# Pacing of weight loads, filler products, narrowing order and MLP piece counts in a DeltaNet + SiLU MLP kernel

## The chip, the cores and the metric

The kernel runs on one core of a Trainium2 chip. Its time is the device time of one execution in microseconds (us); the number given for a kernel is the median of its runs. A core has five engines that work side by side, each through its own instructions in order: TensorE (PE, matrix products; the loads of the stationary operand are shown as PEld), VectorE (DVE), ScalarE (ACT), GpSimd (POOL) and SyncE (SP), which here only issues DMA transfers. The engines wait for each other through semaphores. PE, DVE and ACT meet in PSUM, eight banks that PE writes; everything else lies in SBUF.

## The reference

Two blocks follow each other. The first is a delta rule over 768 tokens, for 4 batches of 8 heads of dimension 48:

```python
k_n = k / (norm(k) + 1e-6)
for t in range(S):
    y[t]  = q[t] @ state
    v_old = state.T @ k_n[t]
    state = state + beta[t] * outer(k_n[t], v[t] - v_old)
```

Its output, as 3072 rows of 384, goes through an MLP: `h = x @ w_in` (384 to 2048), `g = h * sigmoid(h)`, `out = g @ w_out` (2048 to 384). The two weights arrive as 64-bit floats, 6.3 MB each.

## The kernel before, in words

**Chunks.** The 768 tokens are cut into six chunks of 128. In a chunk the recurrence becomes matrix algebra: keys and queries are transposed (`turn`, L412), their products are taken (`score`, L438), a triangular matrix per head is inverted, and then the chunk is solved in two halves (`solve`: `keys`, `inner`, `update`, `old`, `new`, lines L650 to L779). The inversion of chunk 0 (`invert_first`, L549 to L625) works on 16x16 corners on DVE (17 steps, two instructions each), transposes them with DVE and joins them by 32x32 products on PE (L583, L603, L618); that of the later chunks (`invert`, L513/L518) is 31 steps on DVE, after a way through DRAM (`block_out`, `block_in`) and with another one behind it (`low`, `up`, read back by L531 and L100).

**The MLP as filler.** The products of the MLP for chunk c are generators (`feed_forward`: `hidden` L847 and, for chunk 0, `project` L877, later `combine` L944). `run(n)` takes n pieces from them. The main loop calls `run` between the steps of the next chunk's preparation, inversion and solution, so that PE has work while other engines hold up the recurrence. How many pieces stand where is written out by hand.

**Narrowing.** Weights are fetched as pairs of 32-bit words, in 16 pieces of 128x768 doubles (`fetch_w_in` L243, `fetch_w_out` L255), into rooms that are used for something else before or after. `narrow` (L176 to L201) makes a piece into fp32: two ACT instructions (L182, L183), when the piece is begun; then three DVE steps, L187 (maximum), L190 (shift and mask) and L194 (sign), and behind the third one POOL addition (L198). `fill(n)` does the next n of these DVE steps, in the order of a queue of pieces; a piece's ACT instructions are issued by `begin`.

**Order.** Every instruction is pinned behind the one before it on its engine (`pin`), DMA issues on SP too (`in_line`): what a program line issues first runs first on its engine, and what waits holds up all that stands behind it. `behind(a, b, Sync)` makes a wait for b's completion.

**Fillers without a result.** `busy(n)` (L289) issues n products of 128x128 by 384 columns into a bank named `pw` that nobody reads; each shows as two matmul records. `read` (L754) is a copy of eight columns of an accumulating bank, which the next products into that bank wait for.

Of the kernel before, what the change touches and what calls it, by code (L numbers as in the profile page):

```python
# [21 lines left out]
def kernel(  # L22
# [19 lines left out]
    W = 64  # L42
# [26 lines left out]
    def behind(later, earlier, how=NoSync):  # L69

        tc.add_manual_dep(
            later.ins, earlier.ins.name,
            mybir.DependencyInfo(how, mybir.DependencyReason.DATA), reason="order",
        )
# [3 lines left out]
    def pin(op):  # L78

        engine = op.ins.engine  # L80
        if engine in pins:
            behind(op, pins[engine])
        pins[engine] = op
        return op

    line = []

    def in_line(dma):

        if line:  # L90
            behind(dma, line[-1])
        line.append(dma)
        return dma

# [7 lines left out]
    def go(steps, n=1):  # L102
        for _ in range(n):
            next(steps, None)
# [34 lines left out]
    def load_k(c, bs=ALL):  # L139
        if c < NCH:  # L140
            load_pair(kbufs[c % 2], k, c, bs)
# [13 lines left out]
                    ))  # L155

    seen = const.tile([P, 1], FP32, name="seen")
    pin(nc.vector.memset(seen[:], 0.0))
    for t in (kbufs[0], zbuf, kbufs[1]):
        for h in range(2):  # L160
            pin(nc.vector.memset(t[:, 2 * h : 2 * h + 2, :, :, D:W], 0.0))
# [15 lines left out]
    def narrow(to, raw):  # L177

        low, high = raw[..., 0], raw[..., 1]
        bits = to.bitcast(U32)  # L180
        across = "p a f -> p f a"
        pin(nc.scalar.activation(out=to, in_=high.bitcast(FP32), func=ACTF.Abs))  # L182
        pin(nc.scalar.activation(  # L183
            out=low.bitcast(I32), in_=low, func=ACTF.Identity, scale=2.0**-29, bias=plus23[:]
        ))
        yield
        yield pin(nc.vector.tensor_scalar(  # L187
            out=to.rearrange(across), in0=to.rearrange(across), scalar1=LOW_HIGH, scalar2=None, op0=ALU.max
        ))
        yield pin(nc.vector.tensor_scalar(  # L190
            out=bits.rearrange(across), in0=bits.rearrange(across), scalar1=3, scalar2=0x3FFFFFFF,
            op0=ALU.logical_shift_left, op1=ALU.bitwise_and,
        ))
        done = pin(nc.vector.scalar_tensor_tensor(  # L194
            out=bits, in0=high, scalar=0xC0000000, in1=bits,
            op0=ALU.bitwise_and, op1=ALU.bitwise_or,
        ))
        pin(nc.gpsimd.tensor_tensor(  # L198
            out=to.bitcast(I32), in0=to.bitcast(I32), in1=low.bitcast(I32), op=ALU.add
        ))  # L200
        yield done  # L201
# [88 lines left out]
    def busy(n=1, after=None, how=NoSync):  # L290

        for _ in range(n):
            pw = bank(CC, "pw")
            done = pin(nc.tensor.matmul(
                pw[:, 0:DM], lhsT=ident[:],
                rhs=states[0][:].rearrange("p u a w -> p (u a w)")[:, 0:DM], start=True, stop=True,
            ))
            if after is not None:
                behind(done, after, how)
                after = None  # L300
# [4 lines left out]
    def beta_of(c):  # L305
        pb = bank(A, "pb")
        pin(nc.tensor.transpose(
            pb[:, 0:BH], beta_fm[:, c].rearrange("n s t -> n (s t)"), ident[0:BH, 0:BH]
        ))
        pin(nc.scalar.activation(  # L310
            out=beta_tok[:, c, :].rearrange("p (n e) -> p e n", e=2),
            in_=pb[:, 0:BH].rearrange("p (e n) -> p e n", e=2), func=ACTF.Copy,
        ))
# [15 lines left out]
    def add_squares(c, b):  # L329

        pin(nc.vector.tensor_reduce(
            out=sums[c][:, b * H : (b + 1) * H], in_=squared[c, b // HB][:, b % HB], axis=AX.X, op=ALU.add
        ))
# [150 lines left out]
    def block_in(c):  # L484
        there, g, _ = blocks[c]
        in_line(nc.sync.dma_start(out=g, in_=there[:]))
# [257 lines left out]
    def old(c, g, hf):  # L744

        py = pys[g] = bank(A, "pyc")
        for u, p, e, _, of, to in of_heads():
            yield pin(nc.tensor.matmul(  # L748
                py[to, C * p + W * u : C * p + W * (u + 1)],
                lhsT=states[g][of, u, p, :], rhs=kqs[c, g * HB + u][of, p, 1, on(e, hf)],  # L750
                start=p == 0 and u == 0, stop=False, skip_group_check=True,
            ))
        if hf == 1:
            pin(nc.vector.tensor_copy(out=read[:], in_=py[:, 0 : 512 : W]))  # L754

    def new(c, g, hf):

# [247 lines left out]
    class Piece:  # L1005
# [3 lines left out]
        def begin(self):  # L1009
            if self.steps is None:  # L1010
                kind, i = self.name
                self.steps = (narrow_w_in if kind == "in" else narrow_w_out)(i)
                next(self.steps)
# [6 lines left out]
    def fill(n):  # L1020

        for _ in range(n):
            if not queue:
                return
            piece = queue[0]
            piece.begin()
            last = next(piece.steps)
            piece.done += 1
            if piece.done == 3:
                narrowed.append(piece.name)  # L1030
                queue.popleft()
                for i in freed:
                    fetch_w_out(i)
                freed[:] = {
                    ("in", 4): [2], ("in", 5): [3], ("in", 6): [4], ("in", 7): [6], ("out", 0): [7], ("out", 1): [5]
                }.get(piece.name, [])
                for next_up in list(queue)[:2]:
                    if next_up.name in raws:
                        next_up.begin()
        return last  # L1040

    def until(name):
# [31 lines left out]
    def first_queries(b):  # L1074

        def evacuate(j, e, to, of):
            by_act(to, of)

        turn(0, b, 1, M)
        score(0, b, (1,), (A, CC), evacuate)  # L1080

    block_in(0)
    for b in range(2):
        first_queries(b)
    for _ in norm_steps(0):
        pass
    for t in xis:
        pin(nc.gpsimd.memset(t[:], 0.0))
    step = block_steps(0)
    pin(nc.gpsimd.memset(spread[:], 0.0))  # L1090
    for i in range(3):
        fetch_w_in(i)
    for c in range(1, NCH):
        beta_of(c)
    for b in range(2, B):
        first_queries(b)
    for i in range(3):
        begin(("in", i))
    inv = invert_first(step)
    for n in range(1 + Q):  # L1100
        done = next(inv)
        if n in (4, 7, 10, 13):
            busy(1, done, Sync)
    go(inv)
    load_v(0)
    for g in range(2):
        size(0, g)
    for i in (3, 4):
        fetch_w_in(i)
    load_k(1)  # L1110
    for i in (5, 6):
        fetch_w_in(i)
    fill(4)
    go(inv)
    fill(3)
    go(inv)
    fill(1)
    go(inv)
    fetch_w_in(7)
    fill(1)  # L1120
    assert next(inv, 0) == 0

    def masks(g):
        for u in range(HB):
# [28 lines left out]

    def lengths(c):

        for b in range(B):
            square(c, b)
            if b % HB == 1:
                for x in (b - 1, b):
                    add_squares(c, x)  # L1160
                yield
        yield from norm_steps(c)

    def prepare(c):
# [31 lines left out]
    for n in range(5):  # L1196
        go(solving)
        if n in (1, 2):
            masks(n - 1)
        if n > 2:  # L1200
            for b in (0, 1):
                turn(1, 2 * (n - 3) + b, 0, M)
        fill((1, 1, 1, 1, 2)[n])
        busy(1)
    long = lengths(1)
    for n in range(5):
        go(solving)
        run(2)
        if n == 0:
            for i in (0, 1):  # L1210
                fetch_w_out(i)
        fill(2)
        go(long, 2 if n < 2 else 6)
    assert next(solving, 0) == 0
    go(long, 99)
    load_v(1)
# [20 lines left out]
    for c in range(1, NCH):  # L1237
        solving = solve(c)
        long = lengths(c + 1) if c + 1 < NCH else iter(())
        for n in range(6):  # L1240
            go(solving)
            run()
            if n >= 2:
                go(long, 4)
        run(999)
        pieces = chained(feed_forward(c, 0), feed_forward(c, 1))
        needed = iter(())
        go(long, 99)
        for n in range(3):
            go(solving)  # L1250
            run()
            if c == 1:
                go(sums_made)
        assert next(solving, 0) == 0
        if c + 1 < NCH:
            step = block_steps(c + 1)
            for n, _ in enumerate(prepare(c + 1)):
                run(2 if n == 0 else 3 if n == 1 else 1)
                if n == 2:
                    load_v(c + 1)  # L1260
            run(3)
            for n, _ in enumerate(invert(c + 1, step)):
                if n % 7 != 3:
                    run()
                if n == 3:
                    load_k(c + 2)
            run(9)
# [31 lines left out]
```

## Time and profile before

| | |
|---|---|
| runs of the kernel | 757.7, 758.02 and 759.09 us, median 758.02 |
| profiled execution | 760.12 us, of which the profile's span is 758.1 us |
| busy: PE, PEld | 709.8 us (94%), 617.4 us (81%) |
| busy: DVE, ACT, POOL | 414.0 us (55%), 203.8 us (27%), 88.2 us (12%) |
| chain that ended last | PE 70%, DVE 11%, DMA 4% |

Instructions that only issue a DMA, branch or count a semaphore are not in the busy times. A matmul of fp32 is shown as two records, each with a weight load. The granted clock is the share of the full TensorE clock that the core had. In lists of waits the columns are: who waited for whom, microseconds in total, how often, the longest. In timelines: start, duration, engine, line, operation, and in brackets the idle time of the engine just before it and what ended it. In tables by stretch: the stretch and its length, the busy time of PE, PEld, DVE, ACT and POOL with instruction counts, the granted clock, the DMA engines' share and GB/s.

### The profile page before, as it was taken

Reading aid. Unit: us, or ns where it says so; the run is one execution under the profiler, and the core shown is the slowest. Engines: PE = TensorE matmul, PEld = TensorE weight load, DVE = VectorE, ACT = ScalarE, POOL = GpSimd, SP = SyncE. Lnnn points to the kernel's source line nnn. Section 1 sums busy time; section 2 is a strip of 40 time slices with the busy share of each in tenths; the row PEclk is TensorE's granted clock in tenths of the full one; section 3 lists DMA queues with packets and bytes.
Section 4 is the critical chain, followed back from the end, with each engine's and each line's share of the span. In section 5 each row is a group of like instructions: output and inputs, shape, how many; then the busy total and the mean of one; then the engine's idle time right before and its main releaser. Section 6 shows DMA issues by size and latency. Waiting matters only on the chain.

```text
span 758.1 us, 21218 instructions
## 1 busy us (share of the span) xinstructions
PE 709.8 (94%) x9394; PEld 617.4 (81%) x9394; DVE 414.0 (55%) x942; ACT 203.8 (27%) x417; POOL 88.2 (12%) x86
## 2 busy tenths in 40 slices
PE   5779996799999999999999999999999999999996
PEld 4557784476787999897999897999897999989996
DVE  5856877997454493544593543593543593321212
ACT  3514444221233212223212233112233112231110
POOL 4231514600102000102000102000102000000000
PEclk9655999999999999999999999999999999999999
DMA  8951538502117504017504017504017104010000
GB/s 117 283 129 40 169 54 223 83 22 65 32 30 96 91 22 84 3 39 94 94 22 84 6 39 102 84 22 85 6 39 101 42 22 85 9 38 1 22 0 22
DMA packets 149131, 49.25 MB, mean 65 GB/s; under 512 B 134880, under 2 KB 142176, under 8 KB 149040
## 3 DMA queue, kind: packets, MB, share of 16 engines
q1 hardware_dynamic: 146928, 47.63, 31.7%
q8 instruction: 74, 1.21, 0.6%
q10 hardware_dynamic: 2112, 0.26, 0.3%
q14 instruction: 17, 0.14, 0.1%
HBM read 33.91 MB, written 11.80 MB: 60 GB/s over the span
## 4 chain that ended last, share of the span: by engine, by line
PE 70%; DVE 11%; DMA 4%; issue 1%; POOL 1%; ACT 1%; SPq 0%; DVEq 0%; ACTq 0%; POOLq 0%
PE phid L847 27%; PE px L944 14%; PE py L944 9%; PE pyc L761 3%; DMA z<-in_q_dram 3%; PE pa L438 3%; PE pu L707 2%; PE pyc L748 2%; PE ph L675 2%; PE pt L412 2%; PE po L877 2%; PE pz L687 2%; DVE w_out L190 2%; DVE rank L513 2%; DVE x L518 2%; PE px L650 1%
## 5 line engine op out<-in xcount | busy, mean ns | idle before, releaser
L847 PE MATMUL phid<-xT,w_in 128*128 128x256 f32 x1152 | 263.3, 384 | 0.0
L847 PEld LDWEIGHTS phid<-xT,w_in 128*128 128x128 f32 x1152 | 215.8, 191 | 32.3 <-issue 2.8
L857 ACT ACTIVATE gT<-phid 128x512 f32<-128x512 f32 x96 | 57.3, 597 | 193.0 <-PE phid L847 181.3
L513 DVE SCALAR_TENSOR_TENSOR rank<-g,step,x 128x31 f32<-128x31 f32 (+15 forms) x155 | 62.2, 401 | 28.5 <-DMA g<-blocks 24.0
L927 DVE TENSOR_TENSOR sums_of_g<-gT 128x384 f32<-128x384 f32 (+1 forms) x60 | 32.7, 567 | 58.0 <-ACT gT L857 47.3
L944 PE MATMUL px<-sums_of_w,sums_of_g 128*128 128x192 f32 x320 | 58.2, 331 | 0.0
L518 DVE TENSOR_TENSOR x<-x,rank 128x31 f32<-128x31 f32 (+15 forms) x155 | 54.7, 353 | 5.7
L944 PE MATMUL py<-w_out,sums_of_g 128*128 128x192 f32 x320 | 55.3, 326 | 0.0
L944 PEld LDWEIGHTS px<-sums_of_w,sums_of_g 128*128 128x128 f32 x320 | 51.9, 190 | 0.9
L944 PEld LDWEIGHTS py<-w_out,sums_of_g 128*128 128x128 f32 x320 | 52.5, 190 | 0.0
L877 PE MATMUL po<-w_out,gT 128*128 128x384 f32 x128 | 46.0, 505 | 5.5 <-POOL w_out L198 5.5
L327 POOL TENSOR_TENSOR sq<-kb 128x384 f32<-128x384 f32 x24 | 20.5, 876 | 246.8 <-PE px L650 229.4
L687 PEld LDWEIGHTS pz<-vf,xi 64*64 64x64 f32 x768 | 39.8, 141 | 9.3 <-issue 7.1
L687 PE MATMUL pz<-vf,xi 64*64 64x48 f32 x768 | 42.6, 224 | 4.5 <-DVE nt L354 3.8
L448 DVE TENSOR_TENSOR ap<-pa,above 128x256 f32<-128x256 f32 x40 | 15.1, 418 | 51.8 <-ACT ap L453 51.8
L456 DVE COPY xT<-pyc 32x128 f32<-32x128 f32 (+2 forms) x66 | 18.7, 284 | 44.4 <-ACT xT L453 44.4
L877 PEld LDWEIGHTS po<-w_out,gT 128*128 128x128 f32 x128 | 23.7, 194 | 22.5 <-POOL w_out L198 8.0
L438 PE MATMUL pa<-kq 48*64 48x128 f32 (+1 forms) x896 | 29.7, 278 | 7.6 <-ACT kq L422 7.3
L438 PEld LDWEIGHTS pa<-kq 48*64 48x64 f32 x896 | 23.7, 147 | 14.0 <-ACT kq L422 9.0
L748 PE MATMUL pyc<-kq,state 48*64 48x64 f32 x704 | 35.0, 223 | 0.0
L748 PEld LDWEIGHTS pyc<-kq,state 48*64 48x64 f32 x704 | 32.1, 134 | 3.4 <-issue 3.4
L675 PEld LDWEIGHTS ph<-state,kq 48*64 48x64 f32 x704 | 26.7, 134 | 5.0 <-issue 3.8
(159 smaller groups left out, 922.3 us busy)
## 6 DMA issues: line engine op xcount, KB each, us to landing
vf<-in_v_dram SPq DMA_DIRECT2D x24, 192.0 KB, 5.2
out_dram<-o SPq DMA_DIRECT2D x48, 96.0 KB, 2.2
sums_of_w<-in_moe_w_out_dram SPq DMA_DIRECT2D x5, 768.0 KB, 6.2
w_out<-in_moe_w_in_dram SPq DMA_DIRECT2D x4, 768.0 KB, 7.8
blocks<-ap SPq DMA_DIRECT2D x44, 64.0 KB, 1.9
g<-blocks SPq DMA_DIRECT2D x5, 512.0 KB, 3.7
up<-x SPq DMA_DIRECT2D x5, 512.0 KB, 4.0
xi<-up SPq DMA_DIRECT2D x40, 64.0 KB, 2.6
```

What stands on the lines that cost most here:

```text
L438: pin(nc.tensor.matmul(pa[e][half, p * n * W : (p + 1) * n * W], lhsT=kq[rows, p, 0, half], rhs=kq[rows, p, js[0] : js[-1] + 1, half], sta ...
L513: pin(nc.vector.scalar_tensor_tensor(out=tv, in0=g[:, 0:m, m : m + 1].to_broadcast([P, m, n]), scalar=step[:, m : m + 1], in1=x[:, m : m + ...
L518: yield pin(nc.vector.tensor_tensor(out=x[:, 0:m, m:T], in0=x[:, 0:m, m:T], in1=tv, op=ALU.add))
L675: yield pin(nc.tensor.matmul(ph[on(e, hf), n * D : (n + 1) * D], lhsT=kqs[c, g * HB + u][of, p, 0, on(e, hf)], rhs=states[g][of, u, p, 0:D ...
L687: yield pin(nc.tensor.matmul(pz[rows, n * D : (n + 1) * D], lhsT=xis[g][rows, u * H + 2 * p + e, :], rhs=vfs[c][rows, hf, g * HB + u, p, : ...
L748: yield pin(nc.tensor.matmul(py[to, C * p + W * u : C * p + W * (u + 1)], lhsT=states[g][of, u, p, :], rhs=kqs[c, g * HB + u][of, p, 1, on ...
L761: yield pin(nc.tensor.matmul(py[to, C * p + W * u : C * p + W * (u + 1)], lhsT=zbuf[rows, g * HB + u, hf, p, :], rhs=aps[c, g][rows, 1, u, ...
L847: pin(nc.tensor.matmul(ph[:, j * GT : (j + 1) * GT], lhsT=w_in[:, a, (2 * f + j) * P : (2 * f + j + 1) * P], rhs=xTs[c, hf][:, a, :], star ...
L857: pin(nc.scalar.activation(out=gTs[f // FG][:, f % FG, :], in_=ph[:], func=ACTF.Silu, scale=0.5))
L877: pin(nc.tensor.matmul(po[n][:, 0:DM], lhsT=gTs[f // 2 // FG][:, f // 2 % FG, at : at + C], rhs=w_outs[f // HFF][:, f % HFF, :], start=(f ...
L927: pin(nc.vector.tensor_tensor(out=sums_of_g[:, k, fs], in0=of[0], in1=of[1], op=op))
L944: pin(nc.tensor.matmul(to, lhsT=at, rhs=quarter(f, *b) if isinstance(b, tuple) else sums_of_w[b][:, f], start=start and f == 0, stop=f == ...
```

## The change

The lines of the kernel after are one or a few higher than those of before.

- Pacing: `in_line` can make a DMA wait for a DVE instruction (`pace`, filled by `paced`). The chunk-0 values `load_v(0)` go ahead of the weights; `w_in` pieces 2 and 3, the keys of chunk 1 and `w_in` pieces 4 to 7 each wait on SP for the DVE instruction that was last issued at that place. Before, three pieces, the values, two pieces, the keys and two more pieces stood one after another.
- Filler products: four after `block_in(0)`, one after each query block, one ahead of the third; six instead of four beside the chunk-0 inversion, each waiting for a DVE step.
- The scaling of the values (`size`, POOL L397) waits for the DVE instructions that follow the first join (L593).
- Narrowing: L187 and L190 go over the piece in memory order instead of across its rows; `in` 1 and 2 are begun after the inversion; a next piece is begun when the piece ahead has done its first DVE step, instead of two at once when one ends. Fills stand at other places beside the chunk-0 joins.
- `read` is copied by ACT instead of DVE. The squares of a chunk's keys (`lengths`) are taken in two groups, their sums one step later, and in chunk 0's solution the steps of `lengths(1)` come later.
- From chunk 1 on: `run` takes two pieces instead of one in two steps of the solution, three instead of two in the first step of the preparation, and 24 instead of 27 beside the inversion.

```diff
-    line = []
+    line, pace = [], []
     def in_line(dma):
         if line:
             behind(dma, line[-1])
+        if pace:
+            behind(dma, pace.pop(), Sync)
         line.append(dma)
         return dma
...
-    pin(nc.vector.memset(seen[:], 0.0))
+    seen_on = pin(nc.vector.memset(seen[:], 0.0)).ins.engine
...
-        across = "p a f -> p f a"
...
         yield pin(nc.vector.tensor_scalar(
-            out=to.rearrange(across), in0=to.rearrange(across), scalar1=LOW_HIGH, scalar2=None, op0=ALU.max
+            out=to, in0=to, scalar1=LOW_HIGH, scalar2=None, op0=ALU.max
         ))
         yield pin(nc.vector.tensor_scalar(
-            out=bits.rearrange(across), in0=bits.rearrange(across), scalar1=3, scalar2=0x3FFFFFFF,
+            out=bits, in0=bits, scalar1=3, scalar2=0x3FFFFFFF,
...
         if hf == 1:
-            pin(nc.vector.tensor_copy(out=read[:], in_=py[:, 0 : 512 : W]))
+            by_act(read[:], py[:, 0 : 512 : W])
...
-                for next_up in list(queue)[:2]:
-                    if next_up.name in raws:
-                        next_up.begin()
+                if queue and queue[0].name in raws:
+                    queue[0].begin()
+            elif piece.done == 1 and len(queue) > 1 and queue[1].name in raws:
+                queue[1].begin()
...
     block_in(0)
+    busy(4)
     for b in range(2):
         first_queries(b)
+        busy(1)
...
-    for i in range(3):
+    load_v(0)
+    for i in range(2):
         fetch_w_in(i)
     for c in range(1, NCH):
         beta_of(c)
+    busy(1)
     for b in range(2, B):
         first_queries(b)
-    for i in range(3):
-        begin(("in", i))
+        busy(1)
+    begin(("in", 0))
     inv = invert_first(step)
+    def paced(fetch, *args):
+        pace.append(pins[seen_on])
+        fetch(*args)
     for n in range(1 + Q):
         done = next(inv)
-        if n in (4, 7, 10, 13):
+        if n in (6, 8, 10, 12, 13, 14):
             busy(1, done, Sync)
+        if n == 8:
+            paced(fetch_w_in, 2)
+    begin(("in", 1), ("in", 2))
     go(inv)
-    load_v(0)
-    for g in range(2):
-        size(0, g)
-    for i in (3, 4):
-        fetch_w_in(i)
-    load_k(1)
-    for i in (5, 6):
-        fetch_w_in(i)
-    fill(4)
-    go(inv)
+    paced(fetch_w_in, 3)
     fill(3)
     go(inv)
-    fill(1)
+    for g in range(2):
+        size(0, g, pins[seen_on])
+    paced(load_k, 1)
+    fill(2)
     go(inv)
-    fetch_w_in(7)
+    paced(fetch_w_in, 4)
+    fill(2)
+    go(inv)
     fill(1)
     assert next(inv, 0) == 0
+    later = [(fetch_w_in, 5), (fetch_w_in, 6), (fetch_w_in, 7)]
...
     def lengths(c):
-        for b in range(B):
-            square(c, b)
-            if b % HB == 1:
-                for x in (b - 1, b):
-                    add_squares(c, x)
-                yield
+        for g in range(2):
+            for b in range(HB * g, HB * (g + 1)):
+                square(c, b)
+            yield
+            for b in range(HB * g, HB * (g + 1)):
+                add_squares(c, b)
+        yield
         yield from norm_steps(c)
...
+        if n < 3:
+            paced(*later.pop(0))
         fill((1, 1, 1, 1, 2)[n])
...
-        go(long, 2 if n < 2 else 6)
+        go(long, (0, 1, 1, 4, 6)[n])
...
-            run()
+            run(2 if n in (2, 3) else 1)
...
-                run(2 if n == 0 else 3 if n == 1 else 1)
+                run(3 if n < 2 else 1)
...
-                if n % 7 != 3:
+                if n % 4 != 3:
                     run()
```

## The prediction

> **What bounds the kernel now.** I read the totals first, then busy time and granted clock by stretch, then PE's waits stage by stage, and last the timelines of the places that the change touches. Totals and stretches:
>
> ```profile
> span 758.1 us, 21218 instructions
> PE 709.8 (94%) x9394; PEld 617.4 (81%) x9394; DVE 414.0 (55%) x942; ACT 203.8 (27%) x417; POOL 88.2 (12%) x86
> ...
> 18.00:35.50 17.50, 15.31 (x286) 10.05 (x284) 12.95 (x36) 9.90 (x22) 2.40 (x4) 0.58 0.90 255
> 35.50:40.30 4.80, 0.01 (x2) 0.00 (x1) 4.53 (x4) 1.79 (x2) 2.86 (x2) 0.90 0.98 251
> 40.30:73.50 33.20, 30.97 (x859) 23.66 (x860) 18.46 (x26) 10.33 (x17) 7.20 (x5) 0.50 0.30 87
> 107.00:152.00 45.00, 34.44 (x237) 23.15 (x236) 38.12 (x41) 19.15 (x31) 22.54 (x12) 0.96 0.72 148
> ...
> 300.00:417.00 117.00, 114.34 (x1614) 104.43 (x1614) 62.35 (x158) 29.33 (x65) 7.55 (x8) 1.00 0.34 57
> ```
>
> In the later chunks (the last row is one of them) PE is busy 98% at full clock: there only a wait can be won. The room lies ahead of that: 35.5 to 40.3, where PE does nothing; 40.3 to 73.5, where it is busy 93% at a clock of 0.50; and 107 to 152, where DVE (38.1 of 45.0) narrows `w_out`. PE's waits, from 15 to 73 us, 73 to 188 and 188 to 700, and one of ACT's in the second stretch:
>
> ```profile
> PE pl L583 <- issue: 4.8, 1, 4.8
> PE pt L412 <- DMA blocks<-ap: 3.6, 1, 3.6
> PE py L650 <- issue: 1.3, 1, 1.3
> PE pl L618 <- issue: 0.7, 1, 0.7
> PE pl L603 <- issue: 0.2, 1, 0.2
> ...
> PE po L877 <- POOL w_out L198: 5.5, 4, 1.8
> PE pa L438 <- ACT kq L422: 4.5, 1, 4.5
> PE pyc L761 <- DVE read L754: 1.9, 1, 1.9
> ...
> ACT w_out L182 <- POOL w_out L198: 6.4, 1, 6.4
> ...
> PE pt L412 <- DMA z<-in_q_dram: 5.3, 4, 1.4
> PE pz L687 <- DVE nt L354: 3.8, 3, 1.3
> ```
>
> The sum is made against the profiled execution, 760.12 us (span 758.1), which is 2.1 above the median, 758.02. I predict the median, so the differences go onto 758.
>
> **The first join: loads paced, scaling later.** The timeline there, and the record of instruction fetches and of weight pieces:
>
> ```profile
> 32.79 2.01 DVE L575 STREAM_TRANSPOSE sums_of_g<-sums_of_w 128x1024 f32<-128x1024 f32 x1
> ...
> 33.94 3.51 POOL L397 TENSOR_TENSOR vf<-vf,n_slot 128x768 f32<-128x768 f32 x2 [2.65 <-DMA vf<-in_v_dram]
> ...
> 34.68 1.53 DVE L187 TENSOR_SCALAR w_in<-w_in 128x768 f32<-128x768 f32 x1
> ...
> 36.24 2.02 DVE L190 TENSOR_SCALAR w_in<-w_in 128x768 uint32<-128x768 uint32 x1
> ...
> 40.30 1.47 PE L583 MATMUL pl<-sums_of_w,ap 32*32 32x16 f32 x94 [4.79 <-issue]
> ...
> 41.83 0.88 DVE L593 SCALAR_TENSOR_TENSOR sums_of_w<-pl,second,pick 128x256 f32<-128x256 f32 x2 [1.73 <-PE pl L583]
> ```
>
> ```profile
> q8 instruction: 74, 1.21, 0.6%
> ...
> w_out<-in_moe_w_in_dram SPq DMA_DIRECT2D x4, 768.0 KB, 7.8
> ```
>
> PE stops after 34 of the second 128 products of L583 and waits 4.8 us for no semaphore, with the DMA engines at 0.98. Instructions come by a DMA queue too (74 transfers of some 16 KB), so I take this for a fetch that stands behind the loads. After the change only two weight pieces go ahead of the inversion, the third at its step 8 and the others behind the join. The stop then shrinks to about the next largest wait of its kind on a busy queue, 0.7: PE would be ready at about 37.0. DVE, which does three narrowing steps between its transposes and L593, needs 34.80 (end of L575) + 0.93 + 0.90 (L187 and L190 undisturbed, rows below) + 0.96 (L194) = 37.6 and is the later of the two. Against the start of L593 at 41.83 that is 4.2 gained; ends 0 and 4.8.
>
> [...]
>
> Where the pacing may cost: each paced load holds SP's line, so everything behind it waits for the DVE step named. The third weight piece is released near 26.8 us (DVE's step 8) and lands 7.8 later, 34.6, ahead of its ACT step near 41; the fifth lands at 52 to 54, and ACT wants it near 55. I put this at 0, cover 1 to 2 us; were a piece late, each would push DVE, ACT and the joins by as much, so up to +3. The scaling L397 moves behind L593: POOL then no longer runs beside L187 and L190 (1.53 and 2.02 there against 0.92 and 0.86 at best), which is in the sum above; its values are wanted only in the solution, after 61 us.
>
> **The added products and the clock.** Eleven more fillers, each two records:
>
> ```profile
> 47.25 1.65 PE L294 MATMUL pw<-state,ident 128*128 128x384 f32 x2
> 61.49 3.62 PE L650 MATMUL px<-xi,y 32*32 32x32 f32 x128
> ...
> 74.29 0.81 PE L294 MATMUL pw<-state,ident 128*128 128x384 f32 x2
> ...
> 192.70 2.50 PE L650 MATMUL px<-xi,y 32*32 32x32 f32 x128
> ```
>
> They cost 0.8 each at full clock, 1.65 at half: 9 to 18 us of PE, in the 3.6 us wait of PE for `blocks`, in the waits for ACT's key copies, and between DVE's inversion steps, where PE has 17.5 us with little of its own work. I count them at 0 and, if the clock isn't held, at +3, when the last one before the inversion delays its start. They fill PE's gaps while DVE inverts, and the 4.8 us stop ahead of the cold stretch goes. If the clock is then 1.0 from 38 to 73, L650's set of 128 gains 1.1 twice, the five fillers there 0.84 each, 4.2, and the 64x64 and 32x32 products of the joins and the first solution some 2.5: up to 9. DVE and ACT evacuations between them (18.5 and 10.3 us busy in 33) don't shorten, so I take −5; ends 0 and −9.
>
> [...]
>
> **Narrowing order.** Rows by line (count, then ns least/median/most) and an operation of half the length:
>
> ```profile
> L187 DVE TENSOR_SCALAR w_in<-w_in x8: 923/963/1527, 34.7 to 99.5; 128x768 f32<-128x768 f32 x8
> L190 DVE TENSOR_SCALAR w_in<-w_in x8: 859/954/2021, 36.2 to 100.4; 128x768 uint32<-128x768 uint32 x8
> ...
> L190 DVE TENSOR_SCALAR w_out<-w_out x8: 954/2294/3144, 111.3 to 148.6; 128x768 uint32<-128x768 uint32 x8
> L194 DVE SCALAR_TENSOR_TENSOR w_out<-sums_of_w,w_out x5: 957/958/960, 112.4 to 150.9; 128x768 uint32<-128x768 uint32 x5
> ...
> L680 DVE TENSOR_TENSOR vf<-vf,ph x22: 544/553/556, 86.5 to 667.4; 128x384 f32<-128x384 f32 x22
> ```
>
> Across the rows L187 and L190 take 0.96, as much as L194, which has memory order already: by that nothing is gained. Were memory order to bring them near the half-length operation, 0.55, it is 0.4 for each of 16 steps on `w_out`, 6.4; and `w_out`'s L190 is at 2.29 in the median where POOL's L198 runs beside it, 1.3 above its own least, so up to 8.9 if the order also frees it. DVE bounds 107 to 152, so this counts in full; the eight `w_in` pieces have cover. The nearer row is L194, a two-input step; I take a third, −3.0. ends 0 and −8.9 (a longer step is excluded: the same elements without a stride).
>
> **Begin order.** The second piece ahead is begun only when the first has done a step. ACT's L182 then no longer stands in front of ACT's key copies while it waits 6.4 us for POOL: PE's wait of 4.5 goes. Late next is the same L182 in a later place, up to half a POOL addition, 2.2: −2.3 taken; ends 0 and −4.5.
>
> **`read` on ACT.** PE waits 1.9 for DVE's copy, which stands in DVE's line behind narrowing. On ACT, idle most of the time, −1.5; ends 0 and −1.9. The keys' squares in two groups and later steps of `lengths(1)`: the same instructions, beside PE work, 0.
>
> **Piece counts, chunks 1 to 5.** What the moved pieces cover, and what they uncover:
>
> ```profile
> 156.67 20.99 PE L847 MATMUL phid<-xT,w_in 128*128 128x256 f32 x96
> ...
> 296.32 5.34 SPq L100 DMA_DIRECT2D xi<-up  x8
> ...
> 301.71 2.21 PE L650 MATMUL py<-xe,ap 32*32 32x32 f32 x128
> 305.35 2.21 PE L650 MATMUL px<-xi,y 32*32 32x32 f32 x128
> ...
> xi<-up SPq DMA_DIRECT2D x40, 64.0 KB, 2.6
> ```
>
> A piece is 20.99/16 = 1.31 us of PE. Three fewer beside the inversion take 3.9 us of cover; PE's use of `xi` starts at 305.35, the last of its loads is issued at 301.66 and lands 2.6 later, at 304.3, so there is 1.1 to spare and up to 2.8 lost per chunk, 11 over chunks 2 to 5 (chunk 1's inversion ends beside narrowing and other pieces, and isn't counted). The pieces gained cover the wait for `z` (5.3) and `nt` (3.8), 9.1. The two nearly cancel: 0; ends −5 and +8.
>
> **Sum**: −4.2 −5 −3.0 −2.3 −1.5 + 0 = −16.0, 742.
>
> **The rivals.**
> - Clock stays at half and narrowing costs the same. For it: 40 to 73.5 is busy and still at 0.50, and L194. Then −4.2 −2.3 −1.5 = −8: 750.
> - All goes: −4.2 −9 −8.9 −4.5 −1.5 = −28: 730. For it: the 47.25 and 74.29 rows; against: nothing shown in memory order is faster than 0.95. [...]
> - Slower: the paced loads move the queue's pressure onto later instruction fetches. Before, the heaviest loading (0.98) met one fetch, 4.8; later ones met 0.30 and cost 0.2, 0.7 and 1.3, in all 7.0. With loads released at intervals up to 60 us the other three can meet a load each: four at 4.8 are 19.2, 12.2 more, and less narrowing, begin order and `read` (6.8) that is +5.4: 763. It decides from three such stops on (14.4 − 7.0 = 7.4 against 6.8). Against it: one load alone doesn't fill the engines as four did.
> - Cover of `xi` is lost in each chunk, +11, with the first rival's −8: 761. For it: only 1.1 to spare; against: the 9.1 that the pieces cover elsewhere.
> - The gains lie off the path, since something else, such as DVE's remaining 38.1 of 45, ends last all the same: 758. Against it: PE waits for those very steps.
>
> **How the numbers follow.** Chances: main case .45 (its own range 728 to 752), clock stays .20, all goes .11, fetch stops .15, cover lost .05, nothing .04. 0.2%, 1.5 us, is about what a measurement of this kernel can tell from no change. Faster: .45 + .20 + .11 = .76; slower .15 + .05 = .20; same .04. The range 726 to 763 takes in all but the tails.
>
> **What would show it.** PE on L583 without a gap above 1.5 us, and L593 near 37.6; a clock near 1.0 in 38 to 73 and L650's 128 in 2.5; L188 and L191 of the new numbering (L187, L190 here) between 0.55 and 0.95, and without the 2 to 3 us ones; no wait of 4.5 of PE's score on ACT's key copies; `hidden` at full rate some 16 us earlier than at 156.67; in the later chunks smaller waits for `z` and `nt`, and none for `xi`. Wrong it would be through several "issue" waits of 4 us between 30 and 65, a clock still at 0.50, or PE waiting for `xi` in every chunk.

## The result and the profile after

The changed kernel takes 745.56 us (median of 744.64 to 745.76) against 757.86 of the kernel before in the same runs: ratio 0.9836, 95% interval 0.9817 to 0.9854, so 12.3 us faster. In a later set of runs it came to 742.27 against 759.25, ratio 0.9787 (0.9766 to 0.9808). The two intervals don't touch. I therefore take a difference of less than about 0.5% between kernels of different sets as not told apart by times, and go by the profiles there. The sets are: this first one, e1 to e4, e5 to e8, and e9 to e12 (the later set just named), the last on another chip than e1 to e8.

Totals and stretches of the changed kernel, for the same stretches as before:

```profile
span 743.7 us, 21255 instructions
PE 713.0 (96%) x9416; PEld 616.8 (83%) x9416; DVE 392.7 (53%) x930; ACT 204.5 (27%) x429; POOL 82.1 (11%) x86
...
18.00:35.50 17.50, 15.99 (x271) 10.19 (x272) 13.10 (x37) 9.48 (x20) 0.84 (x2) 0.80 0.78 212
35.50:40.30 4.80, 2.81 (x128) 1.65 (x127) 4.27 (x6) 0.08 (x1) 3.21 (x2) 0.72 0.74 201
40.30:73.50 33.20, 28.64 (x808) 22.44 (x812) 17.60 (x25) 11.77 (x19) 7.58 (x6) 0.63 0.49 117
107.00:152.00 45.00, 38.12 (x252) 24.61 (x252) 40.50 (x65) 17.79 (x30) 20.03 (x12) 1.00 0.67 143
```

PE's dead stretch from 35.5 to 40.3 is gone in the main (2.81 busy instead of 0.01), but from 40.3 to 73.5 PE still runs at 0.63 of the clock. DVE's total is 21 us less. PE's waits, for the same three stretches:

```profile
PE pa L439 <- ACT kq L423: 2.7, 4, 0.7
PE py L651 <- issue: 2.7, 1, 2.7
PE pl L604 <- issue: 2.1, 1, 2.1
PE pl L619 <- issue: 0.9, 1, 0.9
PE pl L584 <- issue: 0.8, 1, 0.8
...
PE po L878 <- POOL w_out L199: 2.9, 5, 0.7
PE pt L413 <- DMA z<-in_q_dram: 2.1, 1, 2.1
PE pa L439 <- ACT kq L423: 1.8, 1, 1.8
PE pyc L762 <- ACT read L454: 0.7, 1, 0.7
...
PE pyc L762 <- ACT read L454: 1.0, 2, 0.6
PE phid L848 <- DVE n L361: 0.7, 1, 0.7
PE phid L848 <- DVE o L953: 0.7, 3, 0.2
```

The waits "issue" have not gone, they moved: 4.8, 0.2, 0.7, 1.3 at the joins and the first solution before, 0.8, 2.1, 0.9, 2.7 now. In the later chunks `z` and `nt` are out of the top of the list, and nobody waits for `xi`.

Three marks divide the gain. They are starts: L593/L594 (the first join is done), the first `hidden` product of the MLP, and the first `py` of chunk 1's solution. The first and the last start of a line stand at the end of the rows by line, before and after:

```profile
L847 PE MATMUL phid<-xT,w_in x1152: 379/379/634, 79.6 to 733.3; 128*128 128x256 f32 x192
...
L650 PE MATMUL py<-xe,ap x640: 191/191/212, 187.9 to 642.4; 32*32 32x32 f32 x160
```

```profile
37.42 0.88 DVE L594 SCALAR_TENSOR_TENSOR sums_of_w<-pl,second,pick 128x256 f32<-128x256 f32 x2 [0.47 <-PE pl L584]
...
L848 PE MATMUL phid<-xT,w_in x1152: 379/379/617, 77.4 to 719.3; 128*128 128x256 f32 x192
...
L651 PE MATMUL py<-xe,ap x640: 191/191/212, 176.3 to 625.4; 32*32 32x32 f32 x160
```

The join is 41.83 − 37.42 = 4.4 us earlier, the first MLP product only 2.2, chunk 1's solution 11.6, the end of the span 14.4. So 2.2 of the 4.4 were given back before the MLP began, 9.4 were won between the MLP's start and chunk 1's solution (that stretch fell from 108.3 to 98.9), and 2.8 behind it. (Of the 14.4, the 2.1 by which the profiled execution of before lies above its median are not in the difference of the medians.)

### The profile page after: what moved, and what is told of

It reads as the page before. It is cut to its first block, busy times and chain, and to the rows that moved or that the text cites. A ratio compares the mean times of both kernels' runs of the same rounds, so it can differ in the third digit from the quotient of the medians.

```text
span 743.7 us, 21255 instructions
## 1 busy us (share of the span) xinstructions
PE 713.0 (96%) x9416; PEld 616.8 (83%) x9416; DVE 392.7 (53%) x930; ACT 204.5 (27%) x429; POOL 82.1 (11%) x86
## 5 line engine op out<-in xcount | busy, mean ns | idle before, releaser
L928 DVE TENSOR_TENSOR sums_of_g<-gT 128x384 f32<-128x384 f32 (+1 forms) x60 | 29.3, 510 | 68.2 <-ACT gT L858 57.8
L519 DVE TENSOR_TENSOR x<-x,rank 128x31 f32<-128x31 f32 (+15 forms) x155 | 54.7, 353 | 5.8
L945 PE MATMUL py<-w_out,sums_of_g 128*128 128x192 f32 x320 | 56.9, 329 | 0.0
L439 PE MATMUL pa<-kq 48*64 48x128 f32 (+1 forms) x896 | 27.6, 264 | 4.9 <-ACT kq L423 4.6
L713 DVE TENSOR_TENSOR state<-state,pu 128x384 f32<-128x384 f32 x22 | 12.1, 553 | 36.3 <-PE pu L708 36.2
L439 PEld LDWEIGHTS pa<-kq 48*64 48x64 f32 x896 | 21.9, 136 | 11.1 <-ACT kq L423 6.5
```

The source lines that it names most:

```text
L439: pin(nc.tensor.matmul(pa[e][half, p * n * W : (p + 1) * n * W], lhsT=kq[rows, p, 0, half], rhs=kq[rows, p, js[0] : js[-1] + 1, half], sta ...
L519: yield pin(nc.vector.tensor_tensor(out=x[:, 0:m, m:T], in0=x[:, 0:m, m:T], in1=tv, op=ALU.add))
L928: pin(nc.vector.tensor_tensor(out=sums_of_g[:, k, fs], in0=of[0], in1=of[1], op=op))
L945: pin(nc.tensor.matmul(to, lhsT=at, rhs=quarter(f, *b) if isinstance(b, tuple) else sums_of_w[b][:, f], start=start and f == 0, stop=f == ...
```

## The experiments

e10 is the kernel before with one part of the change, e9 the changed kernel as it is; the others are the changed kernel with one part taken back or altered, and line numbers are its own. The table has, from the same views of each profile, the start of the first `hidden` product, of chunk 1's first `py`, the stretch between them, and the ratio to the kernel before.

| kernel | `hidden` | chunk 1 | between | ratio (95%) |
|---|---|---|---|---|
| before | 79.6 | 187.9 | 108.3 | 1 |
| changed | 77.4 | 176.3 | 98.9 | 0.9836 (0.9817 to 0.9854) |
| e1, rows across | 75.4 | 179.1 | 103.7 | 0.9929 (0.9904 to 0.9953) |
| e2, old piece counts | 76.3 | 175.0 | 98.7 | 0.9869 (0.9843 to 0.9895) |
| e3, old fillers | 77.2 | 177.4 | 100.2 | 0.9839 (0.9823 to 0.9856) |
| e4, loads not paced | 82.3 | 181.4 | 99.1 | 0.9886 (0.9862 to 0.9911) |
| e5, old begin rule | 76.3 | 179.3 | 103.0 | 0.9828 (0.9806 to 0.985) |
| e6, loads moved | 73.2 | 172.1 | 98.9 | 0.9802 (0.9764 to 0.984) |
| e7, five fillers less | 72.7 | 173.6 | 100.9 | 0.9806 (0.9769 to 0.9843) |
| e8, five fillers more | 75.3 | 174.0 | 98.7 | 0.9827 (0.9786 to 0.9867) |
| e9, changed again | 75.6 | 174.7 | 99.1 | 0.9787 (0.9766 to 0.9808) |
| e10, before with memory order | 79.5 | 180.0 | 100.5 | 0.9917 (0.9896 to 0.9938) |
| e11, `read` on DVE | 77.7 | 177.1 | 99.4 | 0.9833 (0.9801 to 0.9866) |
| e12, e6 and e7 | 71.9 | 172.1 | 100.2 | 0.9774 (0.9751 to 0.9797) |

### e1 and e10: the narrowing order

e1 puts the strided order back into the changed kernel:

```diff
-            out=to, in0=to, scalar1=LOW_HIGH, ...
+            out=to.rearrange("p a f -> p f a"), in0=to.rearrange("p a f -> p f a"), scalar1=LOW_HIGH, ...
```

and the same for L191.

> The changed kernel with L188 and L191 across the rows again, all else as changed. Theory (the narrowing order is the largest single gain behind the first join): 0.4 us more for each of the 32 steps, of which those on w_out between 107 and 152 us count; the time rises by 4 to 8 us, to 750 to 753, L188 back at 0.92 and above. Rival (narrowing is covered by PE's pieces, the gain there is the begin order and the read copy): within 1.5 us of 745.6.

e10 takes the order alone, into the kernel before (the reverse edit at L187 and L190).

> Before with L187 and L190 in memory order, and nothing else. Theory (the narrowing order is worth 7 us by itself): 5 to 8 us faster than before, L187 and L190 near 0.55 to 0.7, and the stop of 4.8 us at L583 stays. Rival (it pays only with the new begin order and paced loads): within 2 us of before.

e1 took 754.76 against 759.3: of the changed kernel's gain less than half is left. That is more than the order. Of the 9.6 us by which its profile is longer than the changed kernel's, 4.8 lie between the two marks of the table and 6.8 behind chunk 1's start (its first `hidden` is 2.0 earlier); there PE ran at a clock of 0.50 from 182.9 to 196.5 us, where the changed kernel's profile has it full. The one run of e1 with a mean clock of 0.974 took 749.43, the others, at 0.965 to 0.971, 754 to 756. So e10 is the better measure. It took 752.55 against 759.25, by the ratio 6.3 us faster by itself (4.7 to 7.9), and its first `hidden` starts as before (79.5): all of it is won behind, where the stretch falls from 108.3 to 100.5. Rows by line, of the changed kernel and of e10:

```profile
L188 DVE TENSOR_SCALAR w_in<-w_in x8: 642/684/1270, 34.6 to 95.3; 128x768 f32<-128x768 f32 x8
L188 DVE TENSOR_SCALAR w_out<-w_out x8: 552/554/1826, 107.9 to 136.4; 128x768 f32<-128x768 f32 x8
...
L191 DVE TENSOR_SCALAR w_out<-w_out x8: 551/2071/2242, 108.5 to 137.0; 128x768 uint32<-128x768 uint32 x8
```

```profile
L187 DVE TENSOR_SCALAR w_out<-w_out x8: 553/553/636, 105.2 to 140.3; 128x768 f32<-128x768 f32 x8
L190 DVE TENSOR_SCALAR w_out<-w_out x8: 551/2070/2969, 108.6 to 140.9; 128x768 uint32<-128x768 uint32 x8
```

On `w_out` a step takes 0.55 instead of 0.97 where nothing runs beside it, on `w_in` 0.68. L191 is still at 2.07 in the median. One piece of the changed kernel shows why, in its timeline:

```profile
129.28 0.55 DVE L188 TENSOR_SCALAR w_out<-w_out 128x768 f32<-128x768 f32 x1
129.60 1.95 POOL L199 TENSOR_TENSOR w_out<-w_out,sums_of_w 128x768 int32<-128x768 int32 x1 [1.65 <-DVE w_out L195]
129.87 2.09 DVE L191 TENSOR_SCALAR w_out<-w_out 128x768 uint32<-128x768 uint32 x1
132.00 0.96 DVE L195 SCALAR_TENSOR_TENSOR w_out<-sums_of_w,w_out 128x768 uint32<-128x768 uint32 x1
132.87 0.55 DVE L188 TENSOR_SCALAR w_out<-w_out 128x768 f32<-128x768 f32 x1
```

POOL's addition for the piece before ends at 131.55 and L191 at 131.96, 0.41 later. In all five pieces where L191 begins up to 0.4 behind such an addition it ends 0.41 to 0.43 behind it. From piece to piece it is 3.59 us; two steps of 0.55 and one of 0.96 would be 2.06. So 1.5 us of each such piece are still POOL's, which the order does not touch.

### e4: the loads without their waits

```diff
-            behind(dma, pace.pop(), Sync)
+            behind(dma, pace.pop())
```

> The changed kernel with the paced loads in the same order on SP, but without their wait for a DVE step. Theory (the 4.8 us stop of PE in L583 of before was an instruction fetch behind the loads, and pacing removed it, but put smaller stops of 2.1 and 2.7 us at the keys' and the fifth piece's loads): a stop of 3 to 5 us returns at or near the first join, the later two shrink; 0 to 3 us slower. Rival (the stop belongs to the place in the instruction stream, not to the loads): stops as in the changed kernel, time within 1 us.

750.27 against 759.3, which by the ratios is 4 to 8 us slower than the changed kernel's two sets, more than I had expected. The stop is back where it was, in the timeline of e4:

```profile
34.75 0.29 PE L584 MATMUL pl<-sums_of_w,ap 32*32 32x16 f32 x10
36.65 2.93 SPq L244 DMA_DIRECT2D w_out<-in_moe_w_in_dram  x2
40.15 1.79 PE L584 MATMUL pl<-sums_of_w,ap 32*32 32x16 f32 x118 [5.11 <-issue]
40.15 1.68 PEld L584 LDWEIGHTS pl<-sums_of_w,ap 32*32 32x32 f32 x117 [5.21 <-issue]
41.98 0.88 DVE L594 SCALAR_TENSOR_TENSOR sums_of_w<-pl,second,pick 128x256 f32<-128x256 f32 x2 [5.18 <-PE pl L584]
```

Against the changed kernel the order of every engine's instructions is the same; only SP's waits are gone. PE stops after the same ten products, for 5.1 instead of 0.8 us, and L594 starts 4.6 later. So the 5 us come with the unpaced loads, and pacing leaves 0.8 of them. The stops behind it did not shrink as I had expected: L604's is 3.3, and one of 2.7 has moved to the next set of L651. Chunk 1's solution starts 5.1 later than in the changed kernel.

### e6: three loads moved

```diff
-    paced(load_k, 1)
+    paced(fetch_w_in, 4)
     fill(2)
     go(inv)
-    paced(fetch_w_in, 4)
     fill(2)
...
-    later = [(fetch_w_in, 5), ...
+    later = [(load_k, 1), (fetch_w_in, 5), ...
...
-        if n < 3:
+        if n < 4:
```

> The changed kernel with three loads moved: the fifth w_in piece to where the keys of chunk 1 were issued (38.3 us), the keys and the last three pieces one place later each, so that SP issues nothing between about 45 and 51 us. Theory (PE's 2.7 us stop at L651 is an instruction fetch behind the load issued at 50.96): that stop falls to 1 us or less, L651's second set starts 1.5 to 2 us earlier, 0 to 2 us faster unless the keys come late for the chunk-1 transposes (then a wait of PE pt on kb near 70 us). Rival (the stop belongs to the place in the instruction stream): it stays at 2 to 3.

The stop at L651 stayed, at 2.4 (2.7, and 2.4 in e9), and this time nothing was being loaded. The stretch of the stop in e6, whose last columns are the clock, the DMA share and GB/s:

```profile
50.30:52.90 2.60, 0.20 (x23) 0.09 (x10) 2.45 (x4) 2.15 (x3) 0.98 (x1) 1.00 0.03 6
```

My theory that the load makes this stop falls: with the DMA engines at 0.03, PE stands for 2.4 us all the same.

That the stops are waits for instructions can be read from the instruction queue q8, by its transfers in steps of 0.05 us. Its 74 transfers before are one for every 254 records of PE and PEld, so I take them for PE's. In before, the changed kernel, e4, e6 and e9, each of PE's 19 stops between 30 and 66 us ends 2.3 to 3.2 us behind such a transfer. At the join the transfer came at 37.75 before, 2.2 us after PE had stopped, and at 37.00 in e4, 2.0 after; in the changed kernel it came at 33.75, 1.7 ahead of the stop. The place goes by the number of instructions: e3, with 44 records (22 products) fewer ahead, stops with 97 of L604's 128 products left instead of 120. And from 28 to 63 us no two transfers are less than 3.4 us apart in these five profiles, while 128 products of L584, 256 records, take 1.26 us at full clock: by my estimate from these figures, small products can use up a transfer faster than the next one comes. So a part of these stops (2.4 us in e6) belongs to the place in the instruction stream, and loads lengthen them up to the 5.1 us of e4. L604's stop was 0.9 here against 2.1 and 1.5. `hidden` starts 2.4 to 4.2 us earlier than in the changed kernel's two profiles; the ratio, 0.9802, lies between those of its two sets, so that a gain in time isn't shown.

### e3, e7 and e8: fillers and the clock

e3 takes all the added fillers away (before's `n in (4, 7, 10, 13)`, none behind the block read and the queries). e7 and e8 change the five in the first half of chunk 0's solution, which before has too, to none and to ten (`busy(1)` removed, `busy(2)`).

> The changed kernel with before's filler products only: none behind the first block read and the queries, four beside the first inversion. Theory (the clock of 1.00 from 27 to 37 us is theirs, but the join waits for DVE, and the clock falls back at 37.6 anyway): within 1.5 us of 745.6, clock 0.50 up to about 32 us. Rival (they hold the clock through the first solution): 3 us slower or more.

> The changed kernel without the five filler products of the first half of chunk 0's solution (they are in before too). Theory (the clock stays at 0.50 from 55 to 72 us whatever the fillers do, and at half clock they take 1.65 us each in PE's way): 3 to 6 us faster up to the first hidden product, at the same clock. Rival (they keep the clock from staying low longer): it stays at 0.50 beyond 72 us and the time rises by 2 us or more.

> The changed kernel with those five fillers doubled. Theory (fillers don't bring the clock back earlier): the clock full again only near 72 us or later, 3 to 6 us slower. Rival (products over the whole array bring it back, the small tiles don't): full clock well before 70 us and no more than 2 us slower, or faster.

e3 is at 0.9839, no different from the changed kernel's first set, though 0.5% above its second, and L594 starts at 37.8 against 37.4. The eleven fillers do change the clock ahead of the join; they don't change when DVE ends. The mean clock of e3's four runs is 0.957 to 0.962, that of the changed kernel's eight 0.970 to 0.979: it went up, and the time doesn't show it. Stretches of e3 and, below, of the changed kernel:

```profile
15.00:32.50 17.50, 13.94 (x155) 9.56 (x155) 12.65 (x47) 7.83 (x21) 0.84 (x2) 0.56 0.77 215
```

```profile
20.50:27.40 6.90, 5.89 (x44) 3.54 (x44) 5.45 (x20) 1.76 (x6) 0.00 (x0) 0.51 0.93 175
27.40:37.60 10.20, 9.06 (x305) 6.15 (x306) 9.22 (x19) 6.45 (x9) 1.14 (x2) 1.00 0.69 228
37.60:47.90 10.30, 8.11 (x250) 5.72 (x252) 4.84 (x6) 1.15 (x2) 4.56 (x3) 0.50 0.73 120
47.90:54.70 6.80, 3.13 (x196) 2.33 (x189) 4.32 (x6) 4.11 (x6) 2.65 (x2) 1.00 0.39 114
54.70:71.80 17.10, 17.10 (x355) 13.53 (x349) 10.18 (x16) 5.43 (x9) 2.43 (x2) 0.50 0.37 105
```

At 37.6 the full clock is lost again about when PE's stops begin, returns at 47.9, and is lost a second time behind the 2.7 us stop at L651. Then PE is busy 17.10 of 17.10 us at 0.50. The stretches of this table are 2, 3, 3, 2 and 5 times 3.41 us long. Read in steps of 0.5 us from 12 to 82 us, so it is in all fourteen profiles: from one change of the clock to the next it is always a whole multiple of 3.41 us, from one step (in e9) to ten (in the kernel before). With ten fillers (e8) the clock is 0.77 from 55 to 65 us, that is half for 4.6 us and full from 59.6 on:

```profile
55.00:65.00 10.00, 10.00 (x269) 7.48 (x266) 6.54 (x10) 4.35 (x7) 2.50 (x2) 0.77 0.30 88
65.00:75.00 10.00, 10.00 (x201) 7.38 (x199) 6.37 (x11) 5.43 (x10) 1.85 (x1) 1.00 0.79 244
```

In the changed kernel it came back at 71.8 and, in e9, near 67. So e8 came out as its rival says: the clock is back 7 to 12 us earlier, and `hidden` starts no later (75.3 against 77.4 and 75.6). But the fillers aren't shown to be the cause. In e8 the clock was half without a break from 35.8 on, and had not come back in between. Added up from 33 us to the last return, the half clock lasts 34.1 us before, in e3, e4 and e10, 27.3 to 30.7 in the changed kernel and those with the same fillers and loads there (e1, e2, e5, e9, e11), 23.9 in e8, and 27.3 in e7 with none of the five; it is shortest where the loads are moved, 20.5 in e6 and 17.1 in e12 (from 47.9 on).

In e7 the first `hidden` starts 4.7 us earlier (2.9 earlier than in e9), as its theory had it, since five fillers at half clock (1.65 us each) are out of PE's way; chunk 1's solution starts 2.7 (1.1) earlier, and the ratio, 0.9806, lies between the changed kernel's two. In all three the time is not told apart from the changed kernel's two sets. Where the clock returns differs by 5 us between two profiles of the same kernel, so one profile each is not enough to say what sets it.

### e5 and e11: begin order and `read`

e5 has before's lines back (two pieces begun when one ends), e11 `read` copied by DVE.

> The changed kernel with before's rule for the ACT half of narrowing: when a piece ends, the next two are begun at once. Theory (ACT's two instructions of a piece whose room is still in use stood ahead of the key copies, and gave the 4.5 us wait of PE's score): a wait of 3 to 5 us of PE pa on ACT kq returns between 110 and 130 us, ACT waits for POOL's addition again, 2 to 4 us slower than the changed kernel. Rival (the shorter narrowing steps alone took the wait away): within 1.5 us of it.

> The changed kernel with the copy of the accumulating bank on DVE again. Theory (worth the 1.9 us wait of PE and the small ones of the later chunks, less what is left on ACT): a wait of PE pyc on DVE read of 1 to 2 us returns, 1 us slower, near the limit of what can be told. Rival: no wait returns, since DVE's line is shorter with the contiguous steps; same time.

In e5 PE's wait for the key copies is back at nearly its old size:

```profile
PE pa L439 <- ACT kq L423: 4.0, 1, 4.0
```

and the stretch between `hidden` and chunk 1 is 103.0, 4 us more than in the changed kernel; its ratio, 0.9828, is not told apart. In e10, which has the old rule too, the same wait was 2.2, so the wait depends on where the pieces stand as well. In e11 the wait of PE for `read` is 1.6 instead of 0.7 between 73 and 188 us, 1.1 instead of 1.0 behind: 1 us. In the same set its median is 3.3 us above e9's (0.9833 against 0.9787), but the intervals overlap, so the times don't tell.

### e2: the piece counts

```diff
-            run(2 if n in (2, 3) else 1)
+            run()
...
-                run(3 if n < 2 else 1)
+                run(2 if n == 0 else 3 if n == 1 else 1)
...
-                if n % 4 != 3:
+                if n % 7 != 3:
```

(the last one in the later chunks only).

> The changed kernel with the piece counts of before in chunks 1 to 5 (one piece in each solution step, two and three in the preparation, 27 beside the inversion). Theory (the moved pieces took away the waits for z and nt and cost nothing elsewhere): 3 to 5 us slower, 749 to 751, and the waits for z and nt come back (5.3 and 3.8 us in before). Rival (gain and lost cover cancel, as predicted): within 1.5 us of 745.6.

The waits are back, from 188 to 700 us:

```profile
PE pt L413 <- DMA z<-in_q_dram: 4.5, 4, 1.2
PE pz L688 <- DVE nt L352: 3.1, 3, 1.0
```

From chunk 1's solution to the end of the span e2 needs 569.3 us, before 570.2 and e10, with the same counts, 570.5; the changed kernel 567.4 and 565.9 (e9). Alone this shows little, for the other kernels with the new counts need 566.1 to 570.8 (without e1, whose clock was half there). Clearer is the part between the first `py` of chunk 2 and that of chunk 5: 338.1 to 339.6 us in the three kernels with the old counts, 332.6 to 336.4 in the eleven with the new ones. Behind chunk 5's start 2.5 to 3.6 us of that are given back (120.3 to 121.3 against 117.7 to 117.8), as 16 more PE records stand there (1329 against e2's 1313). So the counts are worth some 2 us; the ratio, 0.9869, says no more. Why no cover was lost shows in the timelines, of the kernel before and of the changed one:

```profile
288.05 0.19 DVE L518 TENSOR_TENSOR x<-x,rank 128x31 f32<-128x31 f32 x1
```

```profile
278.34 0.19 DVE L519 TENSOR_TENSOR x<-x,rank 128x31 f32<-128x31 f32 x1
...
286.57 4.27 SPq L102 DMA_DIRECT2D xi<-up  x8
289.89 2.10 PEld L651 LDWEIGHTS py<-xe,ap 32*32 32x32 f32 x128 [0.23 <-issue]
...
293.53 2.10 PEld L651 LDWEIGHTS px<-xi,y 32*32 32x32 f32 x128 [0.23 <-issue]
```

The read-back of `xi` is issued until 290.84; with the 2.6 of the earlier row it lands at 293.4 by this reckoning, and PE takes it at 293.53 without a wait. It is just in time.

### e9 and e12: the changed kernel again, and a combination

> The changed kernel unchanged, for the spread of its runs and for the same chip as the next ones. Theory: ratio to before within 0.2% of 0.9836; its clock ahead of 75 us may rise and fall at other times than in the first profile, by which single runs differ by some us.

> The changed kernel with the three loads moved and without the five fillers of the first half of chunk 0's solution. Theory (the first hidden product started 4 us earlier with either, for the fillers took PE's time at half clock): chunk 1's solution starts 2 to 5 us earlier than in the changed kernel, 742 to 744 on this scale, ratio to before 0.977 to 0.981. Rival (the DVE-bound stretch behind takes it back): within 1 us of the changed kernel.

In one set of runs the changed kernel took 742.27 (0.9787) and e12 741.01 (0.9774): the same within their intervals. e9 missed its expectation of 0.2%. e12's first `hidden` starts 3.7 us ahead of e9's, chunk 1's solution 2.6, and the span ends 0.8 later; by these figures neither is better. e12's keys came 1.4 us late for PE.

## Why the prediction was right

742.0 was forecast, 745.56 and 742.27 were measured; the sum of 16 is 12.3 (by the medians of the second set 17.0). Its terms did not fare alike.

- **Join, −4.2: right.** L594 starts 4.4 earlier (at 37.4 to 40.0 in all profiles with paced loads), and e4 shows the cause: without the waits the stop is 5.1 and L594 back at 42.0. The instruction transfers bear the mechanism out (e6). PE, not DVE, was the later of the two in the end (L594 waited 0.47 for it). That 0.8 of the stop was left, close to the 0.7 assumed, is luck: the next largest stop before was 1.3, not 0.7, and the 0.7 one came with the DMA engines near idle (0.04 from 48 to 50 us). PE stopped for 5.1 us with loads under way (e4), for 2.4 with the DMA engines at 0.03 (e6).
- **Clock, −5: wrong.** Here the step that failed is that fillers and a shorter stop would hold half of the stretch to 73 us. The clock was lost at 37.6 and again at 54.7, L651's second set takes 3.62 as before, and 2.2 of the join's gain were given back by the first `hidden`. From L594 to the first `hidden` it is 40.0 us (37.8 in e9) against 37.8 before, with 3.5 (2.0) us more of PE's stops; so by my estimate the clock, half for 27.3 us instead of 34.1, gave 1 to 2 us, and the stops took 2 to 3.5. e3 puts the added fillers at nothing that can be told. That fillers and a shorter stop hold the clock was my estimate: the runs show half clock for 27.3 to 30.7 us in the changed kernel and those with its fillers and loads (e1, e2, e5, e9, e11) instead of 34.1, and no run shows the −5. Clock and stops together are worth 0 to +2, not −5; the part of the slower rival that came true is the stops at L604 and L651, 2.1 and 2.7.
- **Narrowing order, −3.0: mis-sized.** e10 measures −6.3. I took a third of the range since L194 was the nearer row; the half-length row, 0.55, was the right one, and its 6.4 came out. The end of −8.9, with L190 freed of POOL, was not reached, as it stays at 2.07; nor does 8.9 follow from the rows given, since 1.3 for each of eight steps would be 10.4 on top of the 6.4.
- **Begin order, −2.3: the right mechanism.** The wait fell from 4.5 to 1.8 and is 4.0 without the rule; its worth in time is not measured beyond the 4 us of the stretch in one profile. The 2.2 set against it is a whole addition of POOL (1.8 to 2.3), not half of one.
- **`read`, −1.5: about 1**, by the waits in e11.
- **Piece counts, 0: mis-sized, about −2.** The waits went as counted. The loss of cover didn't come: from the last inversion step to PE's `py` it was 13.66 us before (288.05 to 301.71) and 11.55 after, 2.1 shorter and not 3.9, and the read-back was issued in 4.27 instead of 5.34. So of the slack of 1.1 some 0.1 is left.
- **Pacing at 0:** the paced pieces were in time; the stops at L604 and L651 come at their issue, but e6 shows that only part of them is theirs.

Two errors of opposite sign, the clock's −5 for 0 to +2 and those of narrowing and the counts, −3 for −6 and 0 for −2, cancel in the main. That the sum came so close is luck; the forecast is better than its terms.

## What to carry to other kernels

An engine that stands still without any releaser may be short of instructions, as PE by this reading was here for 5.1 us in e4 and 2.4 in e6: look at what the DMA engines carry at that moment and at when the instruction queue's transfers come, and let large loads wait until the code-heavy stretch is past (here 0.8 of the 5.1 us were left). Price a changed access order by the fastest row of the same size in the trace as well as by its nearest neighbour, and check what still holds the step, such as another engine's pass over memory (here L191, 2.07 us beside POOL's addition and 0.55 without). Where waits are covered by moving work, compare the place it came from by the two instants that have to meet, not by the work's length.

## What was not expected of the hardware

- In memory order the single-input steps take 0.55 us on pieces of 2x384 elements and 0.68 to 0.69 on 3x256, where nothing runs beside them, against 0.96 for the two-input L195 on as many. Across the rows L187 takes 0.96 in the median on `w_in` and 0.97 on `w_out`. Why the order makes this difference, and why 3x256 takes longer than 2x384, stays open.
- PE stood for 2.4 us behind an instruction transfer with the DMA engines at 0.03 (e6), and no two of these transfers were less than 3.4 us apart (28 to 63 us, five profiles).
- PE busy 17.10 of 17.10 us at half clock (54.7 to 71.8) with 32x32 and 64x64 products and the five fillers, as in the kernel before; what ends it stays open. Every stay at one clock lasted a whole multiple of 3.41 us (12 to 82 us, fourteen profiles).
